# A linear-attention and Fourier feed-forward kernel: first weights loaded and converted ahead of all else, the norm's factor moved into the first batch's states

## Chip, cores and metric

The kernel runs on one core of a Trainium2 chip. The metric is the device time of one execution in microseconds (us). Every run is one launch; the work is fp32, with most products made as three products of split operands (below).

## What is computed

Two layers, one behind the other, on 8 batches of 576 rows:

```python
kv  = einsum('bhsd,bhse->bhde', k, v)        # 8 heads, 64 x 64 states
out = einsum('bhsd,bhde->bhse', q, kv)
rms = sqrt(mean(out * out, -1) + 1e-6)
x   = (out / rms * g_norm)                   # (8, 576, 512), heads side by side
X   = fft(fft(x, axis=1), axis=2)            # rows, then channels
u   = x + real(X)
un  = (u - mean(u)) / sqrt(var(u) + 1e-6)
out = u + relu(un @ w_ch1) @ w_ch2           # 512 -> 2048 -> 512
```

The factor g_norm (64 numbers) multiplies every head's output after the norm. The mean of squares is taken of the output without it. w_ch1 and w_ch2 come as 64-bit floats.

## The kernel before

**Stages of a batch.** For each batch b the states k^T v of 8 heads are formed (`plan_kv`, product at L548, copied to the tile kvt at L559). q is loaded, transposed on PE (L605) and copied (L609). `plan_out` multiplies it with the states in three tiles t of 96 or 97 rows, two sides of the sequence each (L630), into two PSUM banks; ScalarE copies them to x (L645) and squares them in place (L650), VectorE sums the squares (L654), and GpSimd (POOL) multiplies x by g (L665, two per tile). `plan_y` makes 1/rms: a root on ScalarE (L684), a mean on POOL (L687), a reciprocal on VectorE (L690), a refinement on POOL (L694 to L696), a last product on VectorE (L699). `plan_fold` multiplies x with it (L730), folds the channels (L741), makes even and odd parts on POOL (L748) and splits them into a high and a low part (ScalarE L754, POOL L757). `plan_seq` is the transform along the sequence (L772, results split at L786 and L790), `plan_chn` the one along the channels (L807), whose result is mixed (ScalarE L819, VectorE L827) and added to x by POOL (L837, L840, two adds per tile). Then x is stored (L848) and `plan_turn` transposes it (L893) and splits it into the blocks unTh and unTl of 512 tokens (L902, L905).

**Feed-forward.** Nine blocks of 512 tokens, 16 chunks f of 128 hidden channels. The first products (L398, 12 per chunk) and the second ones (L416, 12 per chunk) take split operands: high x high, high x low, low x high. While the batches are worked on, each finished block runs through the first NA = 3 chunks (`plan_early`): three first products with relu, then for each of 4 token tiles the second products of all three chunks. After the batches come the other chunks, packed densely on PE.

**Weights.** A chunk's two weights of 512 KB each (L326) are turned from 64-bit floats to split fp32 pairs by `plan_w`: a clear on ScalarE (L329), five steps on VectorE (L336 to L346), a sum (L937), for w_ch1 also a column sum over four parts (L351, late chunks on POOL), one matmul with a matrix of 1/512 (L359) and a subtraction (L363), then the split (ScalarE L941, L946). Two raw buffers hold loads that are not converted yet.

**Order.** All of this is entered as operations with an engine, a cost in ns and a rank; a list scheduler (`Plan.run`) plays them through and emits the ready operation of lowest rank on each engine, if its buffers are free. Rank is `10 * b + stage` (KV 0, QT 1, OUT 2, SCL 3, FOLD 4, SEQ 5, CHN 6, NRM 7); the evictions of `plan_out` go 20 lower (`r - D1`). Weights have ranks of their own, `W_CONV` for the conversion and `W_RANK` for the loads of f = 0, 1, 2. FFN products of early blocks have rank 1000 and up. A last rank holds filler products of a constant (L468, 60 pairs), which nobody reads. Engines execute in the order emitted; up to 75 us of plan time that order is pinned for the compiler too (`PIN_UNTIL`). An operation marked `port` isn't planned beside a POOL operation. The DMA queue of SP issues nearly all transfers, in the plan's order; v of batch 0 goes through ScalarE's queue. Ring sizes that matter: 8 PSUM banks (p8), 2 states (kvt), 2 raw weights, 8 x tiles.

## Time and profile before

| what | value |
|---|---|
| median of 3 runs | 1024.7 us (1024.18 to 1027.55) |
| the profiled execution | 1024.56 us, its span 1022.8 us |
| granted TensorE clock, mean | 0.997 |
| PE busy | 1003.4 us (98%), 5986 matmuls |
| VectorE (DVE) busy | 475.1 us (46%) |
| ScalarE (ACT) busy | 323.4 us (32%) |
| GpSimd (POOL) busy | 328.5 us (32%) |
| DMA | 140.72 MB, mean 138 GB/s |

How to read the views: times are us from the start of the span. A timeline line has start, length, engine, line, operation, output<-inputs, shapes and a count, and in brackets the idle time before it with what ended it. A group line has the busy sum and the mean ns of one. A line "A:B" of the stretches has the busy us and instruction count of each engine. Matmuls overlap in the pipeline, so a sum of their lengths is more than the time that they take one behind the other, and "busy" counts filler products as well.

### The profile page before, as it was taken

The numbers are of one execution on the slowest core, as the hardware profiler recorded it, in microseconds if no ns is written. First come the engines' busy times: TensorE is split into PE (matmuls) and PEld (weight loads), VectorE is DVE, ScalarE is ACT, GpSimd is POOL, SyncE is SP. The second block draws the span as 40 slices with busy tenths as digits, with TensorE's granted clock in tenths as the row PEclk, the third lists the DMA queues.
The fourth block names the chain that finished last, engine by engine and source line by source line (L and its number), as shares of the span: only waits on it lengthen the run. The fifth ranks groups of instructions, "written<-read, shape, count | busy, mean of one in ns | idle before, by whom it ended". The sixth has DMA issues, their size and how long they took to land.

```text
span 1022.8 us, 15250 instructions
## 1 busy us (share of the span) xinstructions
PE 1003.4 (98%) x5986; PEld 844.7 (83%) x5986; DVE 475.1 (46%) x843; ACT 323.4 (32%) x657; POOL 328.5 (32%) x340
## 2 busy tenths in 40 slices
PE   7998999999999999999999999999999999999997
PEld 5886889899888888888888888888888888888886
DVE  1789776455597869998131313131221311311211
ACT  3565556565544434344221212121121121210110
POOL 1757477765775132235722303020020010100000
PEclk9999999999999999999999999999999999999999
DMA  9999667872246765735552514230320400400101
GB/s 238 236 227 258 184 205 212 219 207 114 88 161 242 268 239 190 250 124 168 163 184 74 181 58 161 82 124 1 127 80 0 165 21 1 165 1 1 42 0 42
DMA packets 109259, 140.72 MB, mean 138 GB/s; under 512 B 51854, under 2 KB 76482, under 8 KB 104580
## 3 DMA queue, kind: packets, MB, share of 16 engines
q1 hardware_dynamic: 105652, 132.28, 41.6%
q0 software_dynamic: 1920, 6.29, 2.0%
q10 hardware_dynamic: 1616, 1.18, 0.4%
q8 instruction: 47, 0.77, 0.3%
q14 instruction: 24, 0.20, 0.1%
HBM read 88.33 MB, written 51.40 MB: 137 GB/s over the span
## 4 chain that ended last, share of the span: by engine, by line
PE 93%; DVE 2%; POOL 2%; DMA 1%; ACT 1%; issue 1%; SPq 0%; DVEq 0%; ACTq 0%; POOLq 0%
PE ps_h L398 39%; PE acc L416 38%; PE ps_o L630 3%; PE ps_f L772 3%; PE ps_f L807 3%; PE ps_k L548 2%; PE ps_s L468 2%; PE ps_q L605 1%; PE ps_t L893 1%; DMA vm<-in_v_dram 1%; POOL x L837 1%; POOL x L665 0%; POOL x L840 0%; DVE x L730 0%; PE ps_w L359 0%
## 5 line engine op out<-in xcount | busy, mean ns | idle before, releaser
L398 PE MATMUL ps_h<-unTh,w 128*128 128x512 f32 x1152 | 357.7, 392 | 2.3 <-DVE ss L654 2.3
L416 PE MATMUL acc<-w,hh 128*128 128x512 f32 x1152 | 346.3, 391 | 0.0
L411 DVE SCALAR_TENSOR_TENSOR hl<-ps_h,hh 128x512 fp32r<-128x512 f32 x144 | 98.9, 687 | 374.0 <-ACT hh L408 373.8
L398 PEld LDWEIGHTS ps_h<-unTh,w 128*128 128x128 f32 x1152 | 215.5, 188 | 46.4 <-DVE ss L654 2.5
L416 PEld LDWEIGHTS acc<-w,hh 128*128 128x128 f32 x1152 | 215.0, 188 | 44.2
L408 ACT ACTIVATE hh<-ps_h 128x512 fp32r<-128x512 f32 x144 | 85.7, 595 | 448.1 <-PE ps_h L398 448.1
L398 PE MATMUL ps_h<-unTl,w 128*128 128x512 f32 x576 | 224.9, 390 | 0.0
L416 PE MATMUL acc<-w,hl 128*128 128x512 f32 x576 | 213.9, 389 | 0.0
L398 PEld LDWEIGHTS ps_h<-unTl,w 128*128 128x128 f32 x576 | 108.6, 189 | 22.8
L416 PEld LDWEIGHTS acc<-w,hl 128*128 128x128 f32 x576 | 108.0, 188 | 22.6
L1218 POOL DMA_INDIRECT uu<-u_scr,rowidx x24 | 23.2, 967 | 285.4 <-DVE uu L1271 176.5
L665 POOL TENSOR_TENSOR x<-x,gb 96x512 f32<-96x512 f32 (+1 forms) x48 | 63.9, 1353 | 76.2 <-ACT x L645 75.1
L1237 POOL TENSOR_TENSOR uu<-uu,up 128x512 f32<-128x512 f32 x36 | 45.6, 1292 | 45.5 <-ACT up L1234 45.5
L654 DVE TENSOR_REDUCE ss<-ps_o 96x8 f32<-96x512 f32 (+1 forms) x48 | 32.1, 683 | 43.4 <-ACT ps_o L650 41.0
L1181 POOL TENSOR_TENSOR w<-wap,w 128x512 fp32r<-128x512 f32 x18 | 26.3, 1463 | 73.8 <-ACT w L1180 73.8
L1271 DVE SCALAR_TENSOR_TENSOR uu<-acc,rs_yb,uu 128x512 f32<-128x512 f32 x36 | 25.2, 743 | 42.5 <-PE acc L416 42.5
L748 POOL TENSOR_TENSOR xe<-ab 96x256 f32<-96x256 f32 (+1 forms) x46 | 35.8, 800 | 23.2 <-DVE ab L741 23.1
L630 PEld LDWEIGHTS ps_o<-kvt,fq 64*96 64x96 f32 (+1 forms) x768 | 36.6, 162 | 4.8 <-issue 2.1
L630 PE MATMUL ps_o<-kvt,fq 64*96 64x64 f32 (+1 forms) x768 | 39.7, 248 | 0.0
L772 PE MATMUL ps_f<-cs,xh 96*128 96x290 f32 (+1 forms) x192 | 39.5, 300 | 0.0
L807 PE MATMUL ps_f<-cd,pt 128*96 128x258 f32 (+1 forms) x288 | 37.0, 284 | 1.0 <-DVE x L730 1.0
L1225 DVE BATCH_NORM_STATS2 bst<-uu 128x6 f32<-128x512 f32 x36 | 24.4, 686 | 28.7 <-DMA uu<-u_scr,rowidx 20.3
(110 smaller groups left out, 1042.8 us busy)
## 6 DMA issues: line engine op xcount, KB each, us to landing
raw<-in_moe_w_ch_dram SPq DMA_DIRECT2D x32, 512.0 KB, 5.7
unT_scr<-unTh SPq DMA_DIRECT2D x9, 1024.0 KB, 4.6
unT_scr<-unTl SPq DMA_DIRECT2D x9, 1024.0 KB
part_scr<-part SPq DMA_DIRECT2D x36, 256.0 KB, 2.9
unTh<-unT_scr SPq DMA_DIRECT2D x9, 1024.0 KB, 4.9
unTl<-unT_scr SPq DMA_DIRECT2D x9, 1024.0 KB, 7.1
up<-part_scr SPq DMA_DIRECT2D x36, 256.0 KB, 2.7
out_dram<-uu SPq DMA_DIRECT2D x36, 256.0 KB, 2.6
```

Of the source, the lines that this page charges most:

```text
L398: nc.tensor.matmul(ps, w[c][:, kc * P : (kc + 1) * P], unT[a][:, kc, :], start=(idx == 0), stop=(idx == 3 * KC - 1),)
L408: nc.scalar.activation(hh, ps, AF.Relu)
L411: nc.vector.scalar_tensor_tensor(hl, ps, 0.0, hh.bitcast(F32), ALU.max, ALU.subtract)
L416: nc.tensor.matmul(acc, hpair[a][:, i * P : (i + 1) * P], w[c], start=(first and n == 0), stop=(last and n == 2),)
L630: nc.tensor.matmul(pss[s].t[:n, at : at + D], fqs[side].t[half, m, :n], kvt.t[half, m], start=True, stop=True,)
L654: nc.vector.tensor_reduce(ss.t[0][:n, :, t, s::2], pss[s].t[:n].rearrange("p (u m e) -> p u m e", u=2, e=D), AX.X, ALU.add,)
L665: nc.gpsimd.tensor_tensor(v_, v_, gb[:n].unsqueeze(1).to_broadcast([n, H, D]), ALU.mult)
L748: nc.gpsimd.tensor_tensor(o[:, s], a[:, 0], a[:, 1], ALU.subtract if s else ALU.add)
L772: nc.tensor.matmul(ps.t[:, :NS], xs[t].t[a][:n, part, ch * P : (ch + 1) * P], cs[:n, part, c, t, :], start=(idx == 0), stop=(idx == 8),)
L807: nc.tensor.matmul(ps.t[:n, :ND], pt.t[a][:, part, ch, offs[t] : offs[t] + n], cd[:, part, c, ch, :], start=(idx == 0), stop=(idx == 5),)
L1181: nc.gpsimd.tensor_tensor(lo, af, hi.bitcast(F32), ALU.subtract)
L1237: nc.gpsimd.tensor_tensor(us[j][i], us[j][i], part, ALU.add)
```

## The change

- The weights of f = 0 get rank -60 for loading and conversion, ahead of everything; those of f = 1 keep load rank 4, with conversion rank 5; f = 2 keeps 11 and 6.
- Batch 0's stages get ranks lower by 40 (-40 to -33), so that nothing of batch 1 or of the other weights stands before them. g_norm's load moves to the rank of batch 0's k and v.
- Batch 0 only: the state is stored twice, as it is (kvt) and times g (kvg, one VectorE multiplication). `plan_out` makes each product twice: from kvt for the squares, from kvg for x. POOL's multiplications of x by g (six) are gone for this batch. The other batches are as before.
- Batch 0 only: the adds of `plan_chn` (six) go from POOL to VectorE.
- Early w_ch1 chunks: no column sum on VectorE; instead four accumulating matmuls with the matrix of 1/512; the planned delay of 2000 ns ahead of them is gone.
- Order pinned to 95 us of plan time instead of 75; 45 pairs of fillers instead of 60; several planned costs changed (they alter the order only).

```diff
-W_CONV = (4, 5, 6)
-W_RANK = (2, 4, 11)
-SPARE = 60
+W_CONV = (-60, 5, 6)
+W_RANK = (-60, 4, 11)
+SPARE = 45
-PIN_UNTIL = 75000
+PIN_UNTIL = 95000
...
-        o = self.op(eng, 600, rank, emit, after, bufs, lag=kb * 4)
+        o = self.op(eng, 600, rank, emit, after, bufs, lag=kb * 4.3)
...
-    def w_mean(ps, total):
-        nc.tensor.matmul(ps[:, :P], mean_t, total, start=True, stop=True)
+    def w_mean(ps, parts):
+        for n, part in enumerate(parts):
+            nc.tensor.matmul(
+                ps[:, :P], mean_t, part, start=(n == 0), stop=(n == len(parts) - 1)
+            )
...
-        return 10 * b + stage
+        return 10 * b + stage - (40 if b == 0 else 0)
...
-    i_gb = dma(32, rank(0, QT), ...)
+    i_gb = dma(32, rank(0, KV), ...)
...
-        return kvt, [done], ld
+        if b:
+            return kvt, kvt, [done], ld
+        kvg = ring("kvt", qkv, [P, NPAIR, D], "kvt")
+        def gain():
+            nc.vector.tensor_tensor(
+                kvg.t, ps.t[:, : NPAIR * D].rearrange("p (c t) -> p c t", c=NPAIR),
+                gb.unsqueeze(1).to_broadcast([P, NPAIR, D]), ALU.mult,
+            )
+        scaled = op("DVE", 330, rank(b, KV), gain, mm + [i_gb], [ps, kvg])
+        return kvt, kvg, [done, scaled], ld
...
+        psg = pss if kvg is kvt else [bank_buf("ps_o") for _ in range(2)]
-        a = op("PE", 1540, r, mm, done, [kvt, x, ss] + pss + fqs)
-        last_qkv.append(a)
+        a = g = op("PE", 1540, r, mm, done, [kvt, x, ss] + pss + fqs)
+        if kvg is not kvt:
+            g = op("PE", 1540, r, lambda: mm(psg, kvg), done, [kvg, x] + psg + fqs)
+        last_qkv.append(g)
...
+        if kvg is not kvt:
+            return ds, [cs_, cs_]
...
+        eng = nc.vector if b == 0 else nc.gpsimd
-            nc.gpsimd.tensor_tensor(xv()[:, :, :W], xv()[:, :, :W], pmv(), ALU.add)
+            eng.tensor_tensor(xv()[:, :, :W], xv()[:, :, :W], pmv(), ALU.add)
...
-        adds = [op("POOL", 1500, r, fn, pms, [x, pm]) for fn in (add_l, add_r)]
+        if b == 0:
+            adds = [op("DVE", 690, r, fn, pms, [x, pm], port=True) for fn in (add_l, add_r)]
+        else:
+            adds = [op("POOL", 1240, r, fn, pms, [x, pm]) for fn in (add_l, add_r)]
...
-                e = op("DVE", 600, r, lambda: w_sum(src.t, pf.t[:, :P]), [e], [src, pf])
-            e = op("PE", 220, r, lambda: w_mean(mean.t, pf.t[:, :P]), [e], [pf, mean], wait=SLACK)
+                e = op(
+                    "PE", 870, r,
+                    lambda: w_mean(mean.t, [src.t[:, c * P : (c + 1) * P] for c in range(KC)]),
+                    [e], [src, mean],
+                )
```

More of the change, by code (lines that the diff above doesn't have):

```diff
@@ L490, in plan_dft @@
                 ))
-        b = op("ACT", 1000, r, lambda: nc.scalar.activation(hi, raw.t[:n, :size], AF.Copy), ld, [raw])
+        b = op("ACT", 100 + size, r, lambda: nc.scalar.activation(hi, raw.t[:n, :size], AF.Copy), ld, [raw])
         c = op(
-            "DVE", 1100, r,
+            "DVE", 200 + 1.6 * size if key == "s" else 200 + size, r,
             lambda: nc.vector.tensor_tensor(lo, raw.t[:n, :size], hi.bitcast(F32), ALU.subtract),
@@ L929, in plan_w @@
         late_ = f >= NA
-        for n, cost in enumerate((620, 620, 700, 620, 700)):
+        for n, cost in enumerate((690, 690, 690, 680, 760)):
             d = op(
```

30 lines of the change are left out of this document (16 added, 14 removed).

## The prediction

> **What bounds the kernel now.** I read the busy time by stretches first, then the same table for the filler matmuls alone, then the timelines of single engines. Columns: stretch, its length, busy us (and count) of PE, its weight loads, DVE, ACT and POOL, granted clock, DMA share, GB/s.
>
> ```profile
> span 1022.8 us, 15250 instructions
> 0.00:20.70 20.70, 13.24 (x145) 11.03 (x146) 0.48 (x4) 4.45 (x9) 0.96 (x9) 1.00 0.97 245
> 20.70:49.80 29.10, 29.10 (x297) 23.34 (x295) 22.23 (x34) 16.59 (x37) 21.92 (x30) 1.00 0.94 233
> 49.80:68.00 18.20, 18.20 (x221) 16.67 (x219) 15.96 (x29) 10.63 (x23) 10.25 (x8) 1.00 0.94 213
> 68.00:94.40 26.40, 21.73 (x260) 18.13 (x258) 24.31 (x37) 16.77 (x40) 16.85 (x20) 1.00 1.05 292
> 94.40:120.00 25.60, 25.57 (x233) 20.95 (x234) 23.83 (x37) 12.99 (x29) 16.04 (x21) 0.93 0.85 197
> 120.00:160.00 40.00, 38.16 (x392) 34.50 (x392) 26.24 (x47) 23.02 (x57) 28.91 (x32) 1.00 0.63 193
> 345.00:1015.00 670.00, 670.00 (x2968) 555.07 (x2968) 239.24 (x421) 138.35 (x236) 120.31 (x102) 1.00 0.31 106
> ```
>
> From 94.4 us PE is nearly never idle, and in 345 to 1015 it is packed. So the end is the sum of PE's needed work plus the time in which PE does none of it, and that time lies before 94.4. Idle is 20.70 - 13.24 = 7.5 in the first stretch and 26.40 - 21.73 = 4.7 in the fourth. "Busy" also hides the fillers, products of a constant that nobody reads (L468); their share by the same stretches:
>
> ```profile
> 0.00:20.70 20.70, 4.13 (x9) 1.96 (x10) 1.00 0.97 245
> 20.70:49.80 29.10, 18.78 (x74) 12.98 (x72) 1.00 0.94 233
> 49.80:68.00 18.20, 1.60 (x6) 0.97 (x6) 1.00 0.94 213
> 68.00:94.40 26.40, 8.91 (x34) 5.63 (x32) 1.00 1.05 292
> ```
>
> 4.1 + 18.8 + 1.6 + 8.9 = 33.4 us, with the idle time 45.6 us lost of the first 94.4. Only this can shrink. It ends when block 0's first FFN product gives PE something to do between the attention products:
>
> ```profile
> 4.85 1.12 PE L548 MATMUL ps_k<-vm,km 128*64 128x64 f32 x16 [4.85 <-DMA vm<-in_v_dram]
> 19.42 1.21 PE L605 MATMUL ps_q<-ident,qt 96*128 96x96 f32 x12
> 26.20 6.65 PE L468 MATMUL ps_s<-still 128*128 128x512 f32 x28
> 49.79 0.54 PE L772 MATMUL ps_f<-cs,xh 97*128 97x290 f32 x2
> 82.85 0.75 DVE L905 TENSOR_TENSOR unTl<-ps_t,unTh 128x84 fp32r<-128x84 f32 x2 [0.82 <-ACT unTh L902]
> 94.43 0.98 PE L398 MATMUL ps_h<-unTh,w 128*128 128x512 f32 x2 [2.33 <-DVE ss L654]
> 94.43 4.61 PE ps_h L398 x12
> 101.36 2.78 PE ps_h L398 x12
> ```
>
> Batch 0 runs as a chain: k and v arrive (4.85), its last q are turned at 19.42, its sequence transform starts at 49.79, block 0 is complete at about 83.6 (the last unTl), and the first product starts at 94.43. The last two lines are the chain of waits: the first 12 products take 4.61 us after the idle gap, against 2.78 later, so 1.8 us more are lost there to a slow restart.
>
> **The change, part by part.** *Weights first.* Both 512 KB loads of f = 0 are now ahead of k on SP's queue; v starts on ScalarE's queue beside them.
>
> ```profile
> 13.79 1.56 SPq L326 DMA_DIRECT2D raw<-in_moe_w_ch_dram  x2
> 43.53 0.40 SPq L326 DMA_DIRECT2D raw<-in_moe_w_ch_dram  x1
> 20.74 0.69 DVE L654 TENSOR_REDUCE ss<-ps_o 97x8 f32<-97x512 f32 x1 [18.90 <-ACT ps_o L650]
> 23.75 0.70 DVE L336 TENSOR_SCALAR ps_a<-ps_a 128x512 f32<-128x512 f32 x1 [0.27 <-ACT ps_a L329]
> 48.36 0.69 DVE L363 TENSOR_TENSOR wa<-wa,ps_w 128x512 f32<-128x512 f32 x1 [3.64 <-PE ps_w L359]
> 57.18 0.68 DVE L946 TENSOR_TENSOR w<-ps_a,w 128x512 fp32r<-128x512 f32 x1
> L351 DVE TENSOR_REDUCE wp<-wa 128x128 f32<-128x512 f32 x3 | 3.3, 1088 | 0.1
> ```
>
> They were issued at 13.79, and what is moved past is k, v and q of batch 0. 1.05 MB at the 245 GB/s of the first stretch is 4.3 us; I take **+4** for batch 0's start (0 if the transfers found free engines, but the share there is 0.97; up to 5.3 at the 197 GB/s of the slowest stretch). For it the conversion leaves the crowded stretch: VectorE waits 18.90 us before its first reduction, and the conversion now spread over 23.75 to 57.9 fits in that hole: 14 steps of 0.7 are 10 us. The column sum (L351, 1.09 each) is gone for f = 0, 1, 2 and paid on PE by three more matmuls of the mean, an estimate of 0.23 to 0.46 us each (once or twice a 512 column product, 2.78 / 12), in filler time. The dropped delay in front of the mean removes waits like the 3.64 at 48.36; if the plan is late by a step or two, PE waits 0.7 to 1.4 us there with batch 0's k/v products queued behind it. The f = 1 loads (before: the first at 43.53) no longer wait for a free raw buffer and now pass batch 1's k and v, which come 4 us later as well; their products then fall into time that the fillers have now (26.20, 6.65 us). Small loads (g_norm ahead of k, sign and order after) cost less than 0.3.
>
> *Norm's factor in the states.* Removed: six multiplications by g on POOL. Added: one VectorE multiplication of the 128x256 state, and each output product twice.
>
> ```profile
> 26.71 5.90 POOL L665 TENSOR_TENSOR x<-x,gb 96x512 f32<-96x512 f32 x4 [1.68 <-ACT x L645]
> 25.09 0.17 DVE L699 TENSOR_TENSOR ps_y<-rs_y,rs_s 97x16 f32<-97x16 f32 x1
> 37.90 0.17 DVE L699 TENSOR_TENSOR ps_y<-rs_y,rs_s 96x16 f32<-96x16 f32 x1
> 37.30 0.68 DVE L494 TENSOR_TENSOR cd<-draw,cd 128x516 fp32r<-128x516 f32 x1
> 23.33 2.94 PE L630 MATMUL ps_o<-kvt,fq 64*96 64x64 f32 x64
> ```
>
> The new multiplication is half of a 516 element one, 0.34 us, and the reductions queue behind it. PE's extra 3 x 1.47 = 4.4 us are covered by the 18.8 us of fillers in 20.7 to 49.8; uncovered they would cost 4.4. Batch 1's k/v products need the second state buffer, which batch 0 holds until its outputs are done; their data come later anyway. Path of batch 0: outputs ended at 26.3; +4 for the loads and +2 for the doubled products (not all 4.4: q's arrival paced the first) give 32.3. Before, y of the last tile stood at 37.9, since the mean stood in POOL's queue behind multiplications until 32.6. The first tile's y came 25.09 - 20.74 = 4.4 after its first reduction began, with two multiplications still in the way; I take 3.7 from the last outputs: 36. From y to the transform it was 49.8 - 37.9 = 11.9, with POOL's queue full; with POOL free I take 7, so the transform starts at **43 instead of 49.8**.
>
> *Order, and adds on VectorE.*
>
> ```profile
> 55.72 1.55 DVE L790 TENSOR_TENSOR pt<-ps_f,pt 128x290 fp32r<-128x290 f32 x4
> 58.77 1.43 PE L807 MATMUL ps_f<-cd,pt 128*97 128x258 f32 x10
> 63.13 1.19 POOL L837 TENSOR_TENSOR x<-x,pm 97x514 f32<-97x514 f32 x1
> 69.32 1.17 POOL L840 TENSOR_TENSOR x<-x,pm 96x510 f32<-96x510 f32 x1
> L741 DVE TENSOR_TENSOR ab<-x 96x512 f32<-96x512 f32 x15 | 20.7, 1388 | 1.1 <-POOL xe L748 1.0
> L741 DVE TENSOR_TENSOR ab<-x 97x512 f32<-97x512 f32 x8 | 5.5, 692 | 0.0
> 89.35 4.42 DVE L741 TENSOR_TENSOR ab<-x 96x512 f32<-96x512 f32 x1
> 91.58 0.52 PE L605 MATMUL ps_q<-ident,qt 96*128 96x96 f32 x4 [1.13 <-ACT xh L754]
> ```
>
> The low halves followed the transform at 55.72 only, behind steps of the weights; batch 0's rank now comes before them, so the channel transform starts 5.8 after the sequence one instead of 9.0: 48.8. The adds: 63.13 to 70.5 on POOL (six of 1.2), now six of 0.69 on VectorE. VectorE's operations with two SBUF inputs show two prices, 0.69 alone (97 rows) and 1.39 on average with POOL at work (96 rows), so 4.1 to 8.3 us; I take 6. They begin some 2 us into the channel transform, and the adds end near 56.5. Turning and splitting took until 83.6, 13 after the adds, with batch 1's evictions and the weights between; with batch 0 first I take 6: block 0 complete at **62.5 instead of 83.6**.
>
> The Trainium skill, page "SBUF — State Buffer", section "Who interferes with whom", speaks against these adds: a VectorE instruction with two SBUF inputs and a GpSimd instruction that reads SBUF exclude each other for a whole instruction. By that rule an add that meets a multiplication pays its length too, an estimate of 0.69 + 1.48 (a quarter of POOL's 5.90), and six of them 13; the 4.42 of 89.35 agrees in kind. By the rule batch 0's path would be 7 us longer than I take it, and the time up to 1020.7 where nothing else fills PE meanwhile; the third rival is its far end.
>
> **Sum.** Up to the start of the transform, lost time was 7.5 + 4.1 + 18.8 = 30.4. The other 19.4 of these 49.8 was needed work; of it some 4.5 (batch 1's q and first output tile, 1.5, and batch 2's first k/v) now comes later. So 43 - 14.9 = 28.1 is lost: **-2.3**, the late start included. From 43 to 62.5 the same kinds of work stand ready as in 49.8 to 68 before, where 1.6 was lost, and the 4.5 besides: 0. From there to 94.4, before lost 8.9 + 4.7 = 13.6 and 1.8 at the restart. Block 0's products fill that: two chunks at 2.78 are 5.6 for sure (their weights are ready or under way), a third and the second products (36, so 3 x 2.78) only when f = 2 is converted, whose loads wait for raw buffers. Between 5.6 and 13.6 I take **-9.5**, and **-1.8** for the restart. What is late next is block 1: its products must replace block 0's after 94.4, where lost time was 25.6 - 25.57 + 40.0 - 38.16 = 1.9; batch 1 starts later (its k and v behind 2.1 MB of weights), so **+3** (0 to 7). The longer pinning (to 95 us of the plan) and the corrected costs change no instruction, only what stands first in a queue; one misplaced instruction costs what PE's waits at 91.58 and 94.43 did, 1.13 and 2.33, and one such pair is in the 3. Fewer fillers (45 pairs for 60) cost or give nothing where PE would be idle anyway. Together -10.6, **-11**. The profiled execution took 1024.56 (span 1022.8); the median of the runs is 1024.7. I forecast 1013.7.
>
> **Rivals.** *VectorE sets the pace up to 120 us.* It is busy 24.3 of 26.4 and 23.8 of 25.6 us there. Then only its saved work counts: 10 of conversion and 3 x 1.09 of column sums moved out, less 6 of adds, 0.3, and its start 4 later (20.74 to 25), 3 in all; with adds at 0.69 each and the wait of 3.64 saved it is 8.5. I take 5: 1019.6. Against it: 6.9 us idle in 20.7 to 49.8 and 2.2 in the next stretch.
>
> *Transfers set the pace.* DMA's share is 0.94 to 1.05 up to 94.4. If data, not order, limit PE there, the same bytes take the same time, and early weights only displace k, v and q: 0 within 3 us, 1024.7. Against it: batch 0's q was all turned by 20.6 us, and its chain ran 63 us longer.
>
> *The adds are blocked.* Place: 50 to 62 us, VectorE's queue of batch 0, while POOL multiplies for batch 1. Price: 4.42 as at 89.35, six times 26.5 instead of 6; block 0 is complete at 83, as before, so nothing fills 62 to 94 and the gains of 2.3, 9.5 and 1.8 are gone; the late start of 4 stays: 1028.6, 1029. It decides from about 4 us an add, where the six cost 24; one such stall in 23 folds speaks against it, VectorE's crowded queue for it.
>
> **How the numbers follow.** Forecast 0.60, VectorE's pace 0.15, transfers 0.10, adds blocked 0.15. The first two are faster by over 0.3% (3.1 us, about what a measurement here can tell): 0.74 with a little taken off; the same 0.11; slower 0.15. Range: the best of the sum is -2.3 - 13.6 - 1.8 with nothing late, -17.7, and 2 more if the late start is hidden, 1005; upward it takes in VectorE's and the transfers' case, 1026, and leaves the blocked adds out.
>
> **What would show it.** First k/v product at 8 to 10 instead of 4.85; conversion done by 20; batch 0's sequence transform at 42 to 45; adds near 0.7 to 1.4; first FFN product at 62 to 70; fillers below 25 us; no idle gap near 91.58 to 94.43. Wrong if the first FFN product comes after 85, if lost time after 94 exceeds 9, or if PE idles past 20 us for k and v.

## The result and the profile after

The changed kernel takes **1032.3 us** (median of five runs, 1030.82 to 1033.71) against 1024.2 for the kernel before on the same chip: ratio 1.0071, 95% interval 1.0057 to 1.0086. It is slower by 0.7% where 1.1% faster was forecast. The profiled execution took 1030.82 us, 6.3 more than the 1024.56 of before. Lines move by 3 to 30 in the new file: PE's k/v products are L551, outputs L646, the sequence transform L793, fillers L471, first FFN products L401; VectorE's folds L762, reductions L673, batch 0's adds L860 and L863.

The busy time by the stretches of the prediction (PE, weight loads, DVE, ACT, POOL, clock, DMA share, GB/s), and behind them the first four stretches for the fillers alone:

```profile
0.00:20.70 20.70, 10.19 (x107) 8.14 (x108) 10.96 (x20) 4.71 (x8) 0.96 (x9) 1.00 0.97 227
20.70:49.80 29.10, 28.73 (x357) 23.53 (x355) 20.23 (x33) 15.12 (x32) 12.18 (x21) 1.00 0.94 219
49.80:68.00 18.20, 18.20 (x196) 17.10 (x195) 16.48 (x29) 9.46 (x22) 3.88 (x4) 1.00 0.79 203
68.00:94.40 26.40, 26.40 (x319) 22.25 (x319) 21.23 (x39) 19.09 (x41) 9.96 (x14) 1.00 1.06 287
94.40:120.00 25.60, 22.46 (x211) 19.45 (x207) 17.74 (x25) 13.32 (x33) 18.66 (x24) 0.87 0.76 177
120.00:160.00 40.00, 37.69 (x430) 34.02 (x428) 26.72 (x45) 23.07 (x54) 31.50 (x34) 1.00 0.72 212
```

```profile
0.00:20.70 20.70, 4.42 (x12) 2.56 (x12) 1.00 0.97 227
20.70:49.80 29.10, 14.53 (x54) 9.53 (x54) 1.00 0.94 219
49.80:68.00 18.20, 3.25 (x12) 2.10 (x12) 1.00 0.79 203
68.00:94.40 26.40, 4.28 (x12) 1.81 (x12) 1.00 1.06 287
```

Add idle time and fillers as the prediction did. Up to 49.8: 20.70 - 10.19 = 10.5 and 29.10 - 28.73 = 0.4 idle, 4.4 + 14.5 fillers, and 4.4 for the outputs that are made twice: 34.2 lost, against 30.4 before. From 49.8 to 68: 3.25 against 1.6. From 68 to 94.4: 4.28 against 13.6, and the slow restart (1.8) is gone. So at 94.4 the change **is ahead, by about 5.7 us**. Then the sign turns: from 94.4 to 160 PE is idle for 3.14 + 2.31 = 5.45 us, against 0.03 + 1.84 = 1.87 before, and the clock column falls to 0.87. As the whole ends 6.3 later, 12.0 us are lost behind 94.4. Two questions follow: why only 5.7 of the forecast 13.6 came, and what takes 12.

Why only 5.7: the timeline of single engines on batch 0's path.

```profile
5.46 0.62 ACT L329 ACTIVATE ps_a<-raw 128x512 f32<-128x512 f32 x1 [2.68 <-DMA raw<-in_moe_w_ch_dram]
5.46 0.92 ACTq L530 DMA_DIRECT2D vm<-in_v_dram  x2
10.51 2.08 PE L360 MATMUL ps_w<-wa,mean_t 128*128 128x128 f32 x8 [10.51 <-DVE wa L963]
14.22 0.96 PE L551 MATMUL ps_k<-vm,km 128*64 128x64 f32 x16
41.50 0.99 DVE L720 TENSOR_TENSOR ps_y<-rs_y,rs_s 96x16 f32<-96x16 f32 x1
44.20 0.69 DVE L337 TENSOR_SCALAR ps_a<-ps_a 128x512 uint32<-128x512 uint32 x1
46.26 0.89 DVE L762 TENSOR_TENSOR part<-x 96x512 f32<-96x512 f32 x1
50.13 0.87 ACT L624 COPY fq<-ps_q 128x388 f32<-128x388 f32 x2 [3.43 <-PE ps_q L620]
50.87 0.64 ACT L775 ACTIVATE xh<-part 96x512 fp32r<-96x512 f32 x1
53.74 0.43 PE L793 MATMUL ps_f<-cs,xh 97*128 97x290 f32 x2
68.71 0.68 DVE L863 TENSOR_TENSOR x<-x,pm 96x510 f32<-96x510 f32 x1
73.36 1.83 DVE L931 TENSOR_TENSOR unTl<-ps_t,unTh 128x300 fp32r<-128x300 f32 x4
79.62 0.73 PE L401 MATMUL ps_h<-unTh,w 128*128 128x512 f32 x2
```

Read it from the left column. ScalarE's first clear for the weights waits 2.68 us for the load; the last two issues of v stand behind it in ScalarE's queue and leave only at 5.46. On PE the matmuls of the weights' mean and some fillers stand ahead of the first k/v product, which starts at 14.22, not 4.85; the section on the prediction takes these 9.4 us apart. y of the last tile is at 41.50; between it and the last fold (46.26) VectorE does steps of f = 1's weights (44.20 is the first of three). The split of that tile (xh, 50.87) stands on ScalarE behind a copy of q that waited 3.43 us for PE. The transform starts at 53.74, later than before (49.79), though block 0's first FFN product comes 14.8 us earlier than before (79.62 against 94.43).

What takes 12, in part: the timeline of VectorE, POOL and PE just behind 94 us, then two stretches with PE's busy time and its clock.

```profile
94.67 5.47 POOL L686 TENSOR_TENSOR x<-x,gb 96x512 f32<-96x512 f32 x4
95.14 3.87 DVE L762 TENSOR_TENSOR ab<-x 96x512 f32<-96x512 f32 x1
98.93 0.68 DVE L673 TENSOR_REDUCE ss<-ps_o 97x8 f32<-97x512 f32 x1
99.66 0.55 PE L620 MATMUL ps_q<-ident,qt 96*128 96x96 f32 x4 [0.74 <-DVE ss L673]
106.19 2.12 PE L646 MATMUL ps_o<-kvt,fq 64*96 64x64 f32 x32 [1.75 <-ACT kvt L562]
```

```profile
103.60:107.00 3.40, 1.65 (x38) 1.44 (x40) 0.07 (x1) 2.54 (x7) 3.26 (x6) 1.00 0.83 211
107.00:113.80 6.80, 6.80 (x38) 5.81 (x36) 3.63 (x6) 2.94 (x7) 3.96 (x6) 0.50 1.09 228
```

One fold takes 3.87 us beside POOL's multiplications (0.69 alone), the reductions stand behind it, PE waits for them. From 103.6 to 107.0 PE is busy for 1.65 of 3.40 us, and in the 6.8 us behind that the granted clock is 0.50. "Busy 6.80" hides this: x38 in 6.80 us.

### The profile page after: what moved, and what is told of

Same layout as the page of the kernel before. It is cut to its first block, busy times and chain, and to the rows that moved or that the text cites. A ratio compares the mean times of both kernels' runs of the same rounds, so it can differ in the third digit from the quotient of the medians.

```text
span 1029.0 us, 15414 instructions
## 1 busy us (share of the span) xinstructions
PE 1006.2 (98%) x6070; PEld 846.1 (82%) x6070; DVE 476.0 (46%) x847; ACT 325.0 (32%) x657; POOL 309.9 (30%) x328
## 4 chain that ended last, share of the span: by engine, by line
PE 91%; DVE 3%; DMA 2%; issue 2%; ACT 1%; POOL 1%; SPq 0%; DVEq 0%; ACTq 0%; POOLq 0%
PE ps_h L401 37%; PE acc L419 36%; PE ps_f L793 4%; PE ps_o L646 3%; PE ps_f L828 3%; PE ps_k L551 2%; PE ps_q L620 2%; PE ps_t L919 2%; PE ps_s L471 1%; DMA part_scr<-part 1%; PE ps_w L360 1%; DMA u_scr<-x 1%; DMA raw<-in_moe_w_ch_dram 0%; DVE x L751 0%; DVE ss L673 0%
## 5 line engine op out<-in xcount | busy, mean ns | idle before, releaser
L401 PE MATMUL ps_h<-unTh,w 128*128 128x512 f32 x1152 | 356.8, 391 | 0.8 <-ACT unTh L928 0.8
L401 PEld LDWEIGHTS ps_h<-unTh,w 128*128 128x128 f32 x1152 | 214.8, 188 | 45.0 <-ACT unTh L928 1.0
L401 PE MATMUL ps_h<-unTl,w 128*128 128x512 f32 x576 | 224.2, 389 | 0.0
L401 PEld LDWEIGHTS ps_h<-unTl,w 128*128 128x128 f32 x576 | 108.1, 188 | 22.5
L686 POOL TENSOR_TENSOR x<-x,gb 96x512 f32<-96x512 f32 (+1 forms) x42 | 54.7, 1325 | 43.3 <-ACT x L663 43.1
L646 PEld LDWEIGHTS ps_o<-kvt,fq 64*96 64x96 f32 (+1 forms) x864 | 42.0, 163 | 7.1 <-issue 2.5
L646 PE MATMUL ps_o<-kvt,fq 64*96 64x64 f32 (+1 forms) x864 | 45.7, 250 | 1.8 <-ACT kvt L562 1.8
L673 DVE TENSOR_REDUCE ss<-ps_o 96x8 f32<-96x512 f32 (+1 forms) x48 | 32.0, 683 | 32.9 <-ACT ps_o L668 32.6
L1211 POOL TENSOR_TENSOR w<-wap,w 128x512 fp32r<-128x512 f32 x18 | 23.2, 1291 | 72.2 <-ACT w L1210 72.2
L931 DVE TENSOR_TENSOR unTl<-ps_t,unTh 128x384 fp32r<-128x384 f32 (+14 forms) x80 | 32.8, 479 | 16.8 <-ACT unTh L928 16.7
L793 PE MATMUL ps_f<-cs,xh 96*128 96x290 f32 (+1 forms) x192 | 39.5, 299 | 0.0
L1255 DVE BATCH_NORM_STATS2 bst<-uu 128x6 f32<-128x512 f32 x36 | 24.5, 686 | 26.5 <-DMA uu<-u_scr,rowidx 18.0
```

The lines of the kernel that those rows point to most:

```text
L401: nc.tensor.matmul(ps, w[c][:, kc * P : (kc + 1) * P], unT[a][:, kc, :], start=(idx == 0), stop=(idx == 3 * KC - 1),)
L646: nc.tensor.matmul(pss[s].t[:n, at : at + D], fqs[side].t[half, m, :n], kvt.t[half, m], start=True, stop=True,)
L673: nc.vector.tensor_reduce(ss.t[0][:n, :, t, s::2], pss[s].t[:n].rearrange("p (u m e) -> p u m e", u=2, e=D), AX.X, ALU.add,)
L686: nc.gpsimd.tensor_tensor(v_, v_, gb[:n].unsqueeze(1).to_broadcast([n, H, D]), ALU.mult)
L793: nc.tensor.matmul(ps.t[:, :NS], xs[t].t[a][:n, part, ch * P : (ch + 1) * P], cs[:n, part, c, t, :], start=(idx == 0), stop=(idx == 8),)
L931: nc.vector.tensor_tensor(unTs[j].t[1][:, :, to], view()[:, :, lo:hi], unTs[j].t[0][:, :, to].bitcast(F32), ALU.subtract,)
```

## The experiments

**How they are compared.** Medians against runs of the kernel before on the same chip. The trace is read by one more number, the time lost: up to a time t, t less what all products done by then take at their packed pace (start to start in packed parts of these traces: FFN product 0.227 us, k/v 0.037 and 0.065, q and turning 0.083, output 0.047, transforms 0.134 and 0.12; fillers and the mean count nothing, batch 0's doubled outputs half). By this count the change is 4.8 us ahead at 95 (5.7 at 94.4 by the busy times, which overlap), and loses 5.9 more than before from 95 to 160, 2.6 to 345 and 2.4 to 500; behind 500 all kernels agree within 0.6. "Half" is the sum of the stretches after 20 us, the end left out, in which the granted clock was 0.5. The us of the second column are medians; the columns from the transform on are read from the one profiled execution of each kernel.

| kernel | us | ratio, 95% | transform | first FFN | lost by 95 / to 160 / to 345 / to 500 | half |
|---|---|---|---|---|---|---|
| before | 1024.2 to 1025.1 | | 49.8 | 94.4 | 49.1 / 7.4 / 5.3 / 2.6 | 3.4 |
| the change | 1032.3 | 1.0071 (1.0057 to 1.0086) | 53.7 | 79.6 | 44.3 / 13.3 / 7.9 / 5.0 | 6.8 |
| e1 weights back | 1025.5 | 1.0001 (0.9990 to 1.0011) | 56.9 | 82.4 | 47.0 / 10.4 / 5.6 / 2.9 | 3.4 |
| e2 gain on POOL | 1029.3 | 1.0030 (1.0013 to 1.0047) | 54.0 | 76.5 | 48.2 / 7.6 / 11.8 / 3.3 | 17.1 |
| e3 adds on POOL | **1018.1** | 0.9930 (0.9910 to 0.9950) | 54.2 | 79.7 | 44.3 / 3.3 / 7.2 / 2.7 | 0 |
| e4 numbers alone | 1028.2 | 1.0030 (1.0017 to 1.0044) | 47.6 | 79.6 | 44.9 / 11.2 / 5.9 / 2.9 | 17.1 |
| e5 planned POOL, run VectorE | 1022.1 | 0.9967 (0.9948 to 0.9985) | 53.9 | 84.3 | 49.1 / 3.2 / 6.9 / 4.4 | 6.8 |
| e6 planned VectorE, run POOL | 1031.0 | 1.0065 (1.0041 to 1.0089) | 54.0 | 79.9 | 44.6 / 13.9 / 8.0 / 4.3 | 6.8 |
| e7 HOP 140 | 1027.3 | 1.0010 (0.9993 to 1.0028) | 51.6 | 76.5 | 43.6 / 9.6 / 14.4 / 3.4 | 13.7 |
| e8 adds POOL, HOP 140 | 1029.8 | 1.0038 (1.0023 to 1.0054) | 51.5 | 78.5 | 43.4 / 8.1 / 15.5 / 2.9 | 13.7 |
| e11 f = 1 later | 1034.5 | 1.0072 (1.0047 to 1.0097) | 50.4 | 82.9 | 42.9 / 15.4 / 13.4 / 2.7 | 20.5 |
| e12 numbers, weights first | 1029.9 | 1.0053 (1.0035 to 1.0071) | 53.0 | 83.7 | 46.4 / 7.7 / 12.6 / 2.6 | 17.1 |
| e13 pinned to the end | 1021.0 | 0.9963 (0.9950 to 0.9975) | 53.7 | 79.6 | 44.3 / 4.4 / 8.7 / 3.3 | 0 |
| e14 e13, folds on POOL | 1027.5 | 1.0031 (1.0020 to 1.0043) | 53.6 | 79.5 | 44.2 / 8.9 / 9.3 / 4.9 | 6.8 |
| e21 e14, one gap filled | 1027.3 | 1.0024 (1.0015 to 1.0033) | 54.0 | 79.9 | 44.5 / 10.0 / 7.8 / 5.3 | 6.8 |
| e17 numbers, pinned | 1031.5 | 1.0066 (1.0047 to 1.0085) | 46.9 | 79.1 | 45.0 / 13.3 / 7.8 / 4.8 | 23.9 |
| e18 adds POOL, pinned | 1019.3 | 0.9945 (0.9930 to 0.9960) | 54.2 | 79.7 | 44.3 / 2.2 / 9.3 / 3.3 | 0 |
| e20 HOP 140, pinned | 1020.3 | 0.9952 (0.9936 to 0.9967) | 52.2 | 77.0 | 44.2 / 3.8 / 9.2 / 3.2 | 0 |
| e23 e18, weights back | 1028.6 | 1.0037 (1.0026 to 1.0049) | 54.6 | 78.8 | 46.3 / 11.3 / 7.9 / 4.7 | 10.2 |
| e24 e18, gain on POOL | 1026.8 | 1.0000 (0.9976 to 1.0024) | 54.2 | 76.0 | 41.4 / 10.5 / 11.5 / 5.0 | 20.5 |

The main theories: the parts themselves cost (the weights ahead of everything, the doubled products, the adds on VectorE); VectorE's folds that POOL blocks cost (S); the order that comes out behind some 65 to 95 us costs, whichever part shifted it (O); and TensorE's clock costs, which falls after thin stretches (C). Each quoted text says what its theories expect.

**One part undone at a time (e1, e2, e3), and the planner's numbers alone on the kernel before (e4).**

```diff
# e1
-W_CONV = (-60, 5, 6)
-W_RANK = (-60, 4, 11)
+W_CONV = (-36, 5, 6)
+W_RANK = (-38, 4, 11)
# e2
-        if b:
+        if b >= 0:
             return kvt, kvt, [done], ld
# e3
-        eng = nc.vector if b == 0 else nc.gpsimd
+        eng = nc.gpsimd
...
-        if b == 0:
+        if b < 0:
             adds = [op("DVE", ...
# e4: before, with SPARE 45, PIN_UNTIL 95000, lag 4.3 and the planned costs of the change
```

> The changed kernel (1032.3 us), with the first weights' loads and conversion put back into the middle of batch 0's stages (load rank -38, conversion rank -36); all else as changed. Theory W (the weights ahead of k, v and q start everything late: lost time of PE at 40 us was 29.2 against 26.7, at 55 us 39.1 against 32.3): PE's first k/v product returns to about 5 us, batch 0's sequence transform to 48 or earlier, and the time falls by 4 to 8, to 1024 to 1028. Rival P (the net loss is the static order that the plan lays out behind 95 us, where the changed kernel lost 13 us to 160 us against 7): the start is earlier but the time stays within 3 of 1032. Rival G (the doubled output products delay batch 0): as P, 1030 to 1033.

> The changed kernel with the norm's factor multiplied by POOL again in batch 0 (no second state, no doubled output products). Theory W: the extra output products lie in filler time and POOL's multiplications come back into batch 0's path, so the time stays or rises: 1032 to 1038, the sequence transform of batch 0 later than 53.7 us by 2 to 6. Rival G: outputs end 4.4 us earlier, the transform starts earlier than 53.7, and the time falls by 3 to 6. Rival P: any change of order moves the time by up to 4 either way, with no tie to the transform's start.

> The changed kernel with batch 0's six adds on POOL again. In the changed kernel's trace the adds took 0.68 each with no stall, 65.2 to 69.4 us. Theory W: block 0 is complete 3 to 4 us later and the time rises by 0 to 3 (1032 to 1035). The forecast's rival (adds blocked by POOL) is ruled out already by 0.68; if it were the cause, the time would fall by 4 or more. Rival P: within 4 either way.

> The kernel before (1024.2 us), with the changed plan's numbers alone: fillers 45 pairs, pinning to 95 us, the new costs and transfer rate; no stage, engine or rank is changed. Theory W: the order shifts a little and the time stays within 3 of 1024. Rival P (the plan's numbers make the order that loses time behind 95 us): 1028 or more, with lost time between 95 and 160 us above 10.

Three undone parts, three gains: 6.8, 3.0 and 14.2 us, 24 together, and the numbers alone lose 3 us. The change as a whole lost 8. If each part had a cost of its own, these would have to add up to 8; so they are not, or not only, costs of the parts. The traces say the same. e1 ends 6.8 sooner, but its transform starts 3.2 us later than in the change, so weights out of batch 0's way did not do it in the way that was thought; its first k/v product came at 8.74, not at 5. In e3 the first 95 us lose the same 44.3 as in the change; all that it gains comes behind, 10.0 us of it from 95 to 160. Its 14.2 us are outside of what each of its theories allowed; a fall of 4 or more was to speak for blocked adds, but at 0.68 each they were not blocked. In e2 rival P came right (3.0, with the transform at 54.0), and so it did in e4 (1028.2, with 11.2 lost from 95 to 160). e4 shows that the planner's numbers alone bring the first FFN product from 94.4 to 79.6, with the transform 2.2 us earlier than before, so the early fill of PE needs none of the other parts; it ends 3 us slower than before all the same.

**Order against engine (e5, e6), and a nudge to the planner (e7, e8).** e5 plans the adds on POOL, as e3, and runs them on VectorE; e6 plans them on VectorE, as the change, and runs them on POOL. HOP is the planner's guess of the time from one engine to another; 140 in place of 150 changes nothing but the order.

```diff
# e5
-        if b == 0:
+        if b < 0:
             adds = [op("DVE", ...
# e6
-        eng = nc.vector if b == 0 else nc.gpsimd
+        eng = nc.gpsimd
# e7 (the change), e8 (e3)
-    HOP = 150
+    HOP = 140
```

> The plan of the kernel with the adds on POOL (1018.1 us), but the six adds are issued on VectorE at the places where that plan issues them: every other instruction of every engine stands in the same order. Theory E (the adds on VectorE themselves cost the 14 us between 1018.1 and 1032.3, by their time on VectorE or by the port): 1028 or more. Theory O (what costs is the order that the planner lays out for everything behind them once the adds stand on another engine; the two kernels had lost the same 44.3 us of PE up to 95 us and differ only later): within 3 of 1018.

> The converse: the changed kernel's plan (1032.3 us), the six adds issued on POOL at the places where that plan issues them, all other instructions in the same order. Theory E: 1018 to 1023. Theory O: within 3 of 1032, or some us above it, since POOL's adds are longer than the plan's.

> The changed kernel with one number of the planner changed that touches no rank and no engine: the hand-over between engines is planned with 140 ns instead of 150. Theory E: the time stays within 2 of 1032. Theory O: the order behind the first stages falls out otherwise and the time moves by 3 or more, either way, with the first 60 us as before (lost time near 39).

> The kernel with the adds on POOL (1018.1 us), planned with 140 ns instead of 150 in the same way. Theory E: within 2 of 1018. Theory O: it moves by 3 or more, most likely up, since 1018 is the best of the orders seen.

The time goes with the plan: e6, with the adds on POOL, stays at 1031.0, within 1.3 us of the change; e5, with the adds on VectorE, takes 1022.1, 10 less than the change and 4 more than e3, just outside of the 3 that O allowed and far from the 1028 of E. The traces confirm that only the adds differ: up to 345 us PE, ScalarE and SP's queue execute in e6 what they execute in the change, in the same order, and in e5 the same as in e3. Ten nanoseconds of HOP move the change by -5 and e3 by +11.7, and both land at 1027 to 1030; in the traces the orders part from some 22 us on. So theory O holds in the main: an order that nobody chose is worth 5 to 12 us, and the engine of the adds, the one part that was moved within an order, 4.0 in e3's and 1.3 or less in the change's.

**The weights' place (e11, e12).** e11 loads and converts the weights of f = 1 and 2 only behind batch 1's k, v and q; e12 puts the first weights ahead in e4.

```diff
# e11
-W_CONV = (-60, 5, 6)
-W_RANK = (-60, 4, 11)
+W_CONV = (-60, 15, 16)
+W_RANK = (-60, 12, 13)
# e12: e4, and
-W_CONV = (4, 5, 6)
-W_RANK = (2, 4, 11)
+W_CONV = (-60, 5, 6)
+W_RANK = (-60, 4, 11)
```

> The changed kernel with the weights of f = 1 and 2 loaded and converted behind batch 1's k, v and q (load ranks 12 and 13, conversion 15 and 16). Theory B (batch 0's path was long because steps of f = 1 stand between its folds on VectorE and its k/v successors wait for 1.05 MB more): the sequence transform starts at 48 to 50 instead of 53.7, batch 1's k/v 4 us earlier than 38.3, lost time at 55 us is 35 or less instead of 39.1. The first FFN chunk starts earlier than 79.6, the second chunk later. Rival (batch 0's path hangs on outputs doubled and on POOL and ScalarE): the transform stays at 52 to 54. The end time tells little, since the order behind falls out otherwise.

> The kernel before with the changed plan's numbers (as in the run with the numbers alone, 1028.2 us, transform at 47.6, first FFN product at 79.6) and the first weights ahead of all else, f = 1 as in the change; no doubled state, no rank change of batch 0, adds on POOL. Theory W: the transform of batch 0 starts 4 us or more later than 47.6, and lost time at 55 us rises from 33.3 to 37 or more; the weights first are the costly part of the early stage. Rival: conversion out of the way makes up for it, the transform at 46 to 49 and the first FFN product before 76.

Both are clear in the first 95 us and gone at the end. With f = 1 and 2 later, the transform starts at 50.4 instead of 53.7: their steps did delay batch 0, by 3.3 us. The first FFN product, expected before 79.6, came at 82.9 all the same. With weights first, the transform goes from 47.6 (e4) to 53.0, 5.4 us later, and the first FFN product from 79.6 to 83.7. Yet e11 is the slowest kernel of all at 1034.5, and e12 is 1.7 above e4.

**The order pinned to the end (e13), and the blocked folds taken away in it (e14).**

```diff
# e13
-PIN_UNTIL = 95000
+PIN_UNTIL = 1000000
# e14: e13, and in plan_fold
-            nc.vector.tensor_tensor(
+            (nc.gpsimd if b else nc.vector).tensor_tensor(
                 two_of(ab), xx ...
```

> The changed kernel with the plan's order pinned to its end instead of to 95 us; no rank, cost or engine is changed. Theory O (the order behind the first stages carries the loss, and from 95 us on it isn't the plan's own): the time moves by 3 or more from 1032.3, and lost time of PE up to 95 us stays near 44. Theory E2 (the loss hangs on what the changed stages cost, whatever the order): within 2 of 1032.

> The kernel pinned to its end, with the folds of batches 1 to 7 issued on POOL instead of VectorE, every other instruction in the same place. A fold reads two SBUF operands; in the changed kernel 23 folds took 14.4 us longer in sum than 0.69 each, the longest 3.87, while POOL multiplied by g. Theory S (VectorE blocked behind POOL's multiplications makes the loss behind 95 us): no fold can block VectorE, lost time from 95 to 345 us falls by 5 or more against the pinned kernel, and the time by 4 to 10. Rival C (half-speed stretches of PE's clock and single late operations): POOL's longer queue (21 folds of about 1.25) eats it, within 3 or slower.

Behind the pin the compiler may reorder what the planner emitted; e13 is the change with the planner's order kept there too. It takes 1021.0: same computation, same first 95 us (44.3 lost in both), **11.3 us less**. In the traces VectorE, ScalarE and POOL execute the same instructions in the same order in both kernels up to 95 us, and in another order behind (SP's queue from 61.8 us on, PE from 121.5). So what the change lost behind 95 us hangs on the compiler's order there, not on what the parts compute. The place is easy to see on VectorE: in the change the fold that takes 3.87 us stands ahead of the reductions (95.14, above); in e13 the reductions go first, and the folds come when POOL's multiplications are over:

```profile
95.02 0.68 DVE L673 TENSOR_REDUCE ss<-ps_o 97x8 f32<-97x512 f32 x1
96.21 1.27 DVE L673 TENSOR_REDUCE ss<-ps_o 97x8 f32<-97x512 f32 x2
98.37 2.35 DVE L762 TENSOR_TENSOR ab<-x 96x512 f32<-96x512 f32 x2
```

That would speak for S, but e14 takes it back. It keeps e13's order and runs the folds of batches 1 to 7 on POOL, where no fold is blocked: the time that VectorE's folds took over 0.69 us each, 9.2 us summed over all folds in e13 (14.3 in the change), is 0.1. The kernel is 6.5 us slower than e13. POOL has 21 folds of 1.27 us more to do in it, so e14 gives no price of a blocked fold, and S is not ruled out as a part of the loss; but a kernel without any gives back 6.5 of the 11.3 us, and among the others the sum doesn't go with the time (e17 has 4.5 us of it and takes 1031.5, e20 6.8 and takes 1020.3). Blocked folds alone don't set the time.

**Filling one gap (e21).** In e14 the clock falls at 106.4, right behind a stretch with one long wait, and once more at 297.6. e21 puts six fillers into that wait and leaves the rest of the order alone.

```diff
+    # in plan_out of batch 3, once, ahead of its first product: 6 times
+    nc.tensor.matmul(pss[0].t, still, still.unsqueeze(1).to_broadcast([P, KC, P]), start=True, stop=True)
```

> The pinned kernel with the later folds on POOL, with six filler multiplications (0.29 us each, 1.8 us in all) put ahead of batch 3's first output product, into the idle time of 2.56 us that this product had at 102.5 to 105.0 behind ACT's copy of k/v; every engine's order is otherwise the same. In that kernel the granted clock fell to half for 3.4 us at 106.4, and half of that, 1.7 us, is the price. Theory C (it is the thinly filled stretch in front that drops the clock): the fall at 106.4 is gone, TensorE's lost time from 95 to 160 us goes from 8.9 to about 7, and the median from 1027.5 to 1025.8. Rival (the clock follows something other than PE's work, or the fillers only push the work behind them back): the fall stays or moves, and the time is 1027.5 to 1029.

PE's timeline and the stretches, first of e14 (two fences), then of e21 (two fences):

```profile
105.03 1.61 PE L646 MATMUL ps_o<-kvt,fq 64*96 64x64 f32 x32 [2.56 <-ACT kvt L562]
```

```profile
103.00:106.40 3.40, 1.37 (x32) 1.37 (x32) 0.00 (x0) 1.51 (x3) 3.40 (x5) 1.00 0.82 229
106.40:109.80 3.40, 3.40 (x19) 2.91 (x16) 1.37 (x2) 2.64 (x5) 3.25 (x5) 0.51 1.12 252
```

```profile
102.74 1.65 PE L641 MATMUL ps_o<-still 128*128 128x512 f32 x6
105.37 1.57 PE L646 MATMUL ps_o<-kvt,fq 64*96 64x64 f32 x32 [0.98 <-ACT kvt L562]
129.19 0.39 PE L919 MATMUL ps_t<-ident,x 96*128 96x96 f32 x2 [0.43 <-POOL x L860]
130.32 0.71 PE L919 MATMUL ps_t<-ident,x 96*128 96x96 f32 x6 [0.75 <-POOL x L863]
```

```profile
103.00:106.40 3.40, 2.42 (x30) 1.81 (x31) 0.00 (x0) 1.48 (x3) 3.40 (x6) 1.00 0.84 235
106.40:109.80 3.40, 3.40 (x32) 2.93 (x29) 1.18 (x2) 2.68 (x6) 3.33 (x4) 1.00 1.10 269
127.70:131.10 3.40, 2.22 (x22) 1.60 (x20) 2.53 (x7) 2.14 (x7) 3.40 (x5) 1.00 1.02 359
131.10:137.90 6.80, 6.80 (x47) 6.10 (x48) 3.17 (x6) 4.63 (x11) 6.66 (x6) 0.50 1.00 346
```

The fall at 106.4 is gone: the granted clock is 1.00 where it was 0.51, and x32 matmuls instead of x19 fall into the same 3.40 us, as theory C expects. The pair alone does not prove it: the fall at 297.6 is gone from e21 as well, where nothing was filled. And the gain did not come: the lost time from 95 to 160 us was to fall from 8.9 to 7 and rose to 10.0, and the median is 1027.3 against 1027.5. The fall has moved, as the rival expects: the clock falls for 6.8 us at 131.1 instead. In front of that the turning waits for POOL's adds, 0.43 and 0.75 us (the last two lines of the timeline of e21). e14 has the very same two waits, 1.2 us later, and kept its clock:

```profile
130.35 0.39 PE L919 MATMUL ps_t<-ident,x 96*128 96x96 f32 x2 [0.43 <-POOL x L860]
131.49 0.72 PE L919 MATMUL ps_t<-ident,x 96*128 96x96 f32 x6 [0.75 <-POOL x L863]
```

The half-speed stretches of all traces are 3.4 us long or whole multiples of it, and within each trace that has several (the one at the kernel's end counted) their starts lie whole multiples of 3.413 us apart, to 0.02 us: e14's 106.44 and 297.59 are 56 such steps apart. So in these traces the clock changes in steps of 3.4 us that run through the whole execution; e21's steps lie 0.8 us off from e14's. Counted in such steps from e14's fall at 106.4, a step ends at 130.3, between the two waits; in e21 the step from 127.7 to 131.1 holds both, and none of the FFN products of 125 to 127. So whether a stretch counts as thin hangs on where the steps lie, and a kernel that is 1.2 us early can lose what it was early by. That it was the steps which made this difference is read from two traces; they were not shifted on purpose.

**What the parts are worth in a pinned order (e17, e18, e20; then e23, e24).** e17 is e4 pinned to the end, e18 is e3 pinned, e20 is e7 pinned; e23 and e24 are e18 with e1's and e2's edit.

> The kernel before with only the planner's numbers of the change (SPARE 45, lag, costs) and the order pinned to the end: no weights first, no gain on the states, the adds on POOL. Unpinned it took 1028.2 with the first FFN product at 79.55 and 20 us of TensorE's time lost from 95 to 500. Theory O (what is lost behind 95 us is the order that is laid out there, and the change's own parts are worth little): the first FFN product stays at 79 to 80, the losses from 95 to 500 fall to 14 to 17 as they did in the change's kernel when pinned, and the median is 1020 to 1024, no worse than the pinned change (1021.0). Rival (the parts, weights first, the gain in the states, VectorE's adds, pay in the end): over 1026.

> The changed kernel with batch 0's adds planned and run on POOL, as in the run that took 1018.1, and the order pinned to the end, as in the run that took 1021.0. If the adds on POOL are a gain in themselves it adds to the pinning's: 1014 to 1017. If each of the two runs was only one good order (theory O), both already lose near to nothing to a half-speed clock and the two do not add: 1017 to 1023, with the first FFN product at 79.7 in either case.

> The changed kernel with HOP 140 in the planner instead of 150 and the order pinned to the end. Nothing that the kernel computes or places differs from the pinned change (1021.0) but the order. Theory O: another order, another time, between 1019 and 1030, which goes with the time lost from 95 to 345 us, and with a half-speed stretch of the clock wherever a 3.4 us window has TensorE's work at 0.3 or less. Rival (pinning as such makes the gain, whatever the order): within 1020 to 1022.

> The changed kernel with batch 0's adds on POOL and the order pinned to the end (1019.3, no idle time of PE over 0.5 us between 95 and 200), with the weights of the first FFN put back behind batch 0's loads (W_CONV -36, W_RANK -38). If weights first is what pays in the pinned kernels (the numbers alone, pinned to the end, took 1031.5): 1023 to 1031, with the first FFN product at 82 instead of 79.7. If the weights pay nothing (rival): 1017 to 1021, with batch 0's transform at 54 or earlier. In either case a half-speed stretch of the clock in mid-run is expected only behind a 3.4 us window in which TensorE's work is at 0.3 or less.

> The same kernel (adds on POOL, pinned to the end, 1019.3) with batch 0's gain multiplied on POOL again, as it was before the change, instead of in the states with a second product for each tile. If the gain in the states pays in the pinned kernels: 1023 to 1031. If it pays nothing (rival): 1017 to 1021; unpinned and with the adds on VectorE this edit gave 1029.3 against 1032.3, 3 us less than the change. The two runs together tell whether one part carries the 12 us by which the numbers alone, pinned (1031.5), stand behind 1019.3, or whether it is the order that each lays out: then both fall outside of what their part can do, in either direction.

e17 failed what O expected of it: 1031.5, not 1020 to 1024. That is what its rival allowed (over 1026). Pinning is no gain in itself; here the order that it kept is 3.3 us slower than the unpinned one. The turning waits 3.19 us for POOL's adds, and the clock is at half for 13.7 us behind it, from 130.0 (and for 10.2 us from 72.0). Its timeline, then its stretch:

```profile
128.30 0.39 PE L893 MATMUL ps_t<-ident,x 97*128 97x97 f32 x2 [3.19 <-POOL x L837]
```

```profile
95.00:160.00 65.00, 60.09 (x598) 53.65 (x596) 42.51 (x80) 35.05 (x81) 43.72 (x51) 0.89 0.65 180
```

e18, the best of this group, has PE busy for the whole of that stretch; the change had this, in the second fence:

```profile
95.00:160.00 65.00, 65.00 (x700) 58.13 (x697) 41.71 (x78) 41.71 (x98) 52.94 (x59) 1.00 0.80 221
```

```profile
95.00:160.00 65.00, 59.55 (x621) 52.97 (x618) 43.86 (x69) 35.80 (x86) 49.55 (x56) 0.95 0.73 199
```

The adds on POOL and the pinning do not add (1018.1, 1021.0, together 1019.3). The change with HOP 140 and pinned is at 1020.3, so under pinning the nudge moved the end by 0.7 where it had moved it by 5 before; that is one pair, 1020.3 is within what both theories of e20 allowed, and e17 shows that it can't be relied on. Taking back the weights (e23) or the gain (e24) costs 9.3 and 7.5 us from e18, while the same two edits *gained* 6.8 and 3.0 from the change. Their sign depends on the kernel that they are made in; most of the loss is from 95 to 160 (9.1 and 8.3 us more than in e18), with half-speed stretches in both. Both times are what the texts expected if the parts pay in a pinned order, but e23's first FFN product came at 78.8, not 82. In e23 one wait is the edit's own: at 98.27 an FFN product waits 2.54 us for VectorE's split of its weights. In e24 a single wait of 1.28 us at 112.2 is followed by 17.1 us at half speed, and its two fastest executions (1020.0 and 1020.3, with a mean granted clock of 0.999) are within 1 us of e18. So a price for weights first or for the gain in the states can't be read from the end time, and the texts on e23 and e24 did not tell the parts from the order; what can be read is the first 95 us, in which e23 loses 2.0 us more than e18 and e24 2.9 less.

**What the table says as a whole.** The four kernels without a half-speed stretch in the middle take 1018.1 to 1021.0; all others take 1022.1 to 1034.5. The same shows between executions of one program, whose order is fixed: e24's take from 1020.0 us (mean granted clock 0.999) to 1029.3 (0.987), e5's from 1017.9 (0.999) to 1026.0 (0.994). A stretch of waits costs its idle time and, when it is thin enough, half of the half-speed time behind it. The change's 6.8 us cost 3.4, of the 12 lost behind 94.4. The rest is waits and thinly filled stretches spread over the order, without a single place.

## Why the prediction was wrong

Two terms of the sum failed. The gain up to 94.4 us, -13.6, came out at -5.7, since batch 0 started and ran later than the sum had it; and the +3 for what stands behind 94.4 came out at +12.0, which is the order there. The second decided the sign.

**What bounds the kernel.** Right up to 94.4 us, wrong as a bound: "only this can shrink" left out that what lay behind 94.4, nearly without idle time, could grow. It grew by 12.0.

**Weights first, +4.** The first k/v product came at 14.22 instead of 8 to 10, 9.4 us later than before. The weights' loads alone give 4.8 of this, near the +4: 9.49 in e12 against 4.71 in e4. The rest, 4.7, was priced at under 0.3 for g_norm's load ahead of k, and at 0.7 to 1.4 for a late mean on PE. First the kernel before, then e1 (two lines), e12 (two lines) and the change:

```profile
0.00:4.80 4.80, 0.00 (x0) 0.00 (x0) 0.48 (x4) 1.49 (x2) 0.96 (x9) 1.00 0.57 159
```

```profile
0.00:4.80 4.80, 0.00 (x0) 0.00 (x0) 0.48 (x4) 1.49 (x2) 0.96 (x9) 1.00 0.17 45
8.74 1.12 PE L551 MATMUL ps_k<-vm,km 128*64 128x64 f32 x16 [8.74 <-DMA km<-in_k_dram]
```

```profile
4.80:8.70 3.90, 0.00 (x0) 0.00 (x0) 2.39 (x4) 1.24 (x2) 0.00 (x0) 1.00 1.11 309
9.49 1.12 PE L548 MATMUL ps_k<-vm,km 128*64 128x64 f32 x16 [9.49 <-DMA km<-in_k_dram]
```

```profile
4.80:8.70 3.90, 0.00 (x0) 0.00 (x0) 2.49 (x4) 1.24 (x2) 0.00 (x0) 1.00 0.69 228
```

g_norm's 32 KB are not cheap there. In e1 and e23, where they are first in SP's queue and the weights come later, the first k/v product waits for k until 8.74 and 8.96 us; where g_norm comes behind k (before, e4, e17) it starts at 4.85, 4.71 and 4.92. In the first 4.8 us the transfers run at 45 and 40 GB/s in e1 and e23, and at 159 to 163 in the other three. In the change g_norm's load stands between the weights and k, and from 4.8 to 8.7 us 228 GB/s are moved, against 309 in e12 with the same weights ahead and g_norm behind. On PE, the mean's matmuls, which wait for VectorE until 10.51, and four fillers stand ahead of the product. How the 4.7 us split between the two is not shown: no run moved g_norm's load alone. v's last issues, which left at 5.46 behind ScalarE's waiting clear, left as late in e12 (5.56), so they are not the difference. On the transform the weights cost 5.4 (e12 against e4). Conversion done by 20: right, the last step ends at 18.66.

**y at 36, transform at 43.** This step failed, by 5.5 and then by 5.2 more: 41.50 and 53.74. The outputs ended at 35.0 instead of 32.3, so 2.7 of the 5.5 come from the late start; y came 6.5 behind them instead of 3.7, behind VectorE's split of a transform matrix (39.04 to 40.97) and a weights step. I took 7 us from y to the transform "with POOL free". POOL was free (12.18 busy, before 21.92); VectorE's steps of f = 1 and ScalarE's queue took its place. 3.3 us of it are shown to be the weights of f = 1 and 2 (e11); ScalarE's wait is read from the trace only. In the sum: up to 68 us, 5.5 lost more than before instead of 2.3 less.

**Adds on VectorE, 6 us.** Right and on the safe side: six of 0.68, none blocked, from 65.19 to 69.4. The rival of blocked adds did not happen, and the expected 6 us from there to block 0's completion were 5.8. The Trainium skill's rule of the page "SBUF — State Buffer", "Who interferes with whom", is borne out by the folds (3.87 beside POOL's four multiplications, 5.47 together), not by the adds, which met no multiplication: POOL was busy for 3.88 us from 49.8 to 68.

**Block 0's products, -9.5, and the restart, -1.8.** The lost time from 68 to 94.4 fell from 13.6 to 4.28: 9.3, as forecast (-9.5), though the first product came at 79.62 instead of 62.5; the number is luck in part, since until 79.62 other products than block 0's filled the place. And e4 shows that the planner's numbers alone bring this early product, where I had put it down to the parts. Fillers, expected below 25 us, were 26.5.

**Block 1 late, +3 (0 to 7).** This is the term that decides, and it measured +12.0: 3.6 more idle and 1.7 more of half-speed clock from 94.4 to 160. By the lost time, which counts as lost what a busy PE does slowly, it is 5.9 from 95 to 160 and 5.0 from 160 to 500. I had priced one late batch and "one misplaced instruction". e13, with the same first 95 us, and e5 to e8 show that this term is the order behind 95 us and the clock that goes with it: with the same 5.7 us won up to 94.4, it comes to about -1 in e3 (1017.77 in the profiled execution), +2.4 in e13 (1021.28) and +12 in the change. Of the sentence "the longer pinning and the corrected costs change no instruction, only what stands first in a queue", the first half is right and the second half is the whole result. The sum that I gave, -13.6 and +3, is -5.7 and +12.0.

**The rivals.** VectorE's pace and the transfers were not it: PE's fill from 68 to 94.4 came as forecast, though transfers did set batch 0's start. The slower end that I named had the wrong mechanism. My own bound for "wrong" was right: lost time after 94 over 9.

**Open.** Which waits make up the 5.0 us between 160 and 500; why pinning helps the change and not e17; what g_norm's load ahead of k costs by itself. The kernel before with its own order pinned to the end was not run. e7, e24 and e2 spread over 1022.4 to 1031.3, 1020.0 to 1029.3 and 1024.4 to 1031.1 in one program, in e24 and e2 with the granted clock (0.999 to 0.987, 0.996 to 0.990); steps of the clock that lie differently from execution to execution would do that, but only one execution of each was profiled.

## What to carry to other kernels

When an edit goes through a scheduler, it changes the order of everything behind it; before a gain or a loss is put down to the edit, nudge the scheduler by a number that means nothing and see how far the time moves (here 5 to 12 us, where the whole change came out at 8). Compare kernels in stretches, and trust an edit's effect only where the order is the same on both sides. What was won early is kept only if the part behind it keeps PE filled: the two best kernels here (1018.1 with the adds back on POOL, 1019.3 with the order pinned besides) are the change's first 95 us with no long wait from 95 to 200.
